# Making Q-hat and K-hat one turn earlier, with the gate row on GpSimd and value tiles that keep their zeros

## The chip, the cores and the metric

The kernel runs on one core of a Trainium2 chip. The metric is the device time of one execution in microseconds (us). The kernel before takes 488.94 us (median of 4 runs, 488.67 to 490.05).

Engine names: TensorE (PE, with its weight loads PEld), VectorE (DVE), ScalarE (ACT), GpSimd (POOL), SyncE (SP), which issues most transfers.

## The reference, cut to what matters

```python
# for each batch b, head h: a complex decay per position and feature
scale = np.minimum(mag, 0.999) / (mag + 1e-06)
a_re_n, a_im_n = a_re * scale, a_im * scale
for t in range(S):                                   # S = 768, D = 48, B = 4, H = 8
    new_re = ar * S_re - ai * S_im
    new_im = ar * S_im + ai * S_re
    S_re, S_im = new_re + k[t] (x) v[t], new_im
    y[t] = q[t] @ S_re
# then y, as 3072 rows of 384, goes through a mixture of 8 experts (one per row)
```

## The kernel before

The scan is done in chunks of 128 positions. A unit is one chunk of one batch (24 units); two units are a group. For each group the kernel makes logarithms and angles of the decays, sums them along the chunk with a triangular matmul (`ls` for the logarithms, `u` for the angles), and takes exponentials (`pm`, the moduli) and sines (`cs`). ScalarE needs one table of functions for exponentials and another for sines and arctangents (the traces show a table load of 1.28 us at each change), so these come in two blocks that alternate from turn to turn. VectorE multiplies them into q and k, which gives Q-hat and K-hat, the "hats". TensorE transposes the hats, forms their products `wp`, and multiplies these with V.

```python
    def hats(x, i):                    # group x, unit i of it
        P = un.tile([L, H, 2, D], F32, name="P")
        nc.vector.tensor_tensor(P[:], cs[:, i], both(pm[:, 0, i]), Alu.mult)
        kp = un.tile([L, H, D], F32, name="kp")
        nc.vector.tensor_tensor(kp[:], qk[:, 1, i], pm[:, 1, i], Alu.mult)
        for u in range(2):             # the last row of P is the gate of the whole chunk
            nc.sync.dma_start(out=c_scr[g * B + b, u][None], in_=P[L - 1:L]...)
        Qh = un.tile([L, H, 2, D], F32, name="Qh", bufs=3)
        nc.vector.tensor_tensor(Qh[:], P[:], both(qk[:, 0, i]), Alu.mult)
        KW = un.tile([L, H, C + L], F32, name="KW", bufs=5)
        nc.vector.tensor_tensor(KW[:, :, 0:C]..., cs[:, i], both(kp[:]), Alu.mult)
    # [cut]
    for w in range(NU + 1):            # one turn per unit
        unit(values, w + 1)            # loads of V and of the gate row, broadcast (cB)
        unit(turned, w + 2)            # transposes tKT, tQT on TensorE
        unit(inner, w + 1)             # wp, masked by VectorE into KW
        unit(outer, w)                 # py; U and the state update (GpSimd: t1, t2, state)
        unit(rows, w - 1)              # xw, xr
        if w % NG == 0:
            trigs(w // NG + 2)         # sines; arctangent; matmul sums u; squares
        else:
            exps(w // NG + 2)          # matmul sums ls; moduli pm; logarithms
        hat(w + 3)
```

The order in which the program names the operations is not quite the order on an engine. A scheduler puts each engine's operations in a fixed order before the run.

## Time and profile before

| | kernel before |
|---|---|
| time, 4 runs | 488.94 us (488.67 to 490.05) |
| span of the first profile | 467.5 us (this run itself: 469.34 us) |
| span of a second profile, other chip | 485.5 us |
| first product of the experts begins | 373.9 us, and 373.8 us |
| from there to the end | 93.6 us, and 111.7 us |
| TensorE waits at the transposes for K-hat | 46.9 us, and 47.4 us |

The prediction shows the views of the first profile that matter: busy shares, waits, the chain, and stretches of two turns each.

### The profile page before, as it was taken

The page shows a single profiled execution, that of the slowest core. Times are in us where ns is not written, and L with a number is a line of the kernel's source. Part 1 is how long each engine was busy: PE and PEld are TensorE (multiplying, and loading weights), DVE is VectorE, ACT ScalarE, POOL GpSimd, SP SyncE. Part 2 cuts the span into 40 slices and gives each one's busy share as a digit, 9 for nine tenths or more (in the row PEclk, how much of TensorE's full clock was granted, in tenths as well). Part 3 has the DMA queues.
Part 4 walks back from the last instruction along what each step waited for, and adds up shares of the span by engine and source line. Part 5 has one row for each costly group of instructions (what it writes and reads, how often), then busy time and mean ns, then how long its engine had stood idle before and what let it go on. Part 6 is the DMA issues. An engine that isn't in the chain of part 4 may idle for free.

```text
span 467.5 us, 8629 instructions
## 1 busy us (share of the span) xinstructions
PE 356.8 (76%) x3141; PEld 276.6 (59%) x3141; DVE 283.0 (61%) x563; ACT 263.7 (56%) x440; POOL 188.9 (40%) x218
## 2 busy tenths in 40 slices
PE   0356547386979879796969799796993199999994
PEld 0134415265767667674748577685882078777773
DVE  2586754657769687897766667946347034344441
ACT  3485956587869685866958675634521233333332
POOL 5521051634345445346332504133000647776542
PEclk9978777788898989797999979897997589999999
DMA  9949399289596969495919646517201999999991
GB/s 152 187 71 146 64 195 194 49 159 179 114 161 110 186 123 174 78 195 97 175 47 170 111 89 133 71 36 129 48 18 25 378 389 402 395 407 405 408 401 44
DMA packets 159500, 80.84 MB, mean 173 GB/s; under 512 B 135551, under 2 KB 149876, under 8 KB 159458
## 3 DMA queue, kind: packets, MB, share of 16 engines
q1 hardware_dynamic: 144466, 59.92, 52.1%
q0 software_dynamic: 14992, 20.37, 22.6%
q8 instruction: 25, 0.41, 0.4%
q14 instruction: 17, 0.14, 0.1%
HBM read 85.68 MB, written 21.12 MB: 228 GB/s over the span
## 4 chain that ended last, share of the span: by engine, by line
PE 58%; DVE 11%; issue 10%; ACT 8%; DMA 5%; POOL 4%; SPq 2%; POOLq 0%; DVEq 0%; ACTq 0%
PE wp L211 10%; PE py L235 8%; PE tKT L201 6%; PE h_ps L658 6%; PE tQT L201 5%; PE y_ps L669 5%; PE xw L263 5%; PE u L137 4%; PE py L238 4%; DVE KW L179 3%; PE tz L223 2%; POOL out_dram L677 2%; DMA ab<-in_a_im_dram 2%; DVE P L171 2%; DVE kp L173 2%
## 5 line engine op out<-in xcount | busy, mean ns | idle before, releaser
L201 PE MATMUL tKT<-ident,KW 128*96 128x128 f32 x192 | 35.9, 347 | 53.8 <-DVE KW L179 46.9
L201 PEld LDWEIGHTS tKT<-ident,KW 128*96 128x96 f32 x192 | 28.2, 161 | 63.6 <-issue 44.0
L235 PE MATMUL py<-KW,V 128*64 128x224 f32 x384 | 56.0, 358 | 0.0
L184 POOL MEMSET V<- 128x128 f32 x24 | 4.9, 207 | 121.2 <-PE py L235 121.2
L211 PE MATMUL wp<-QT,KT 96*64 96x128 f32 x768 | 53.2, 297 | 0.0
L211 PEld LDWEIGHTS wp<-QT,KT 96*64 96x64 f32 x768 | 47.4, 152 | 6.4 <-issue 2.9
L137 PE MATMUL u<-tan,turn 128*128 128x384 f32 x48 | 25.3, 615 | 34.0 <-ACT tan L82 34.0
L114 POOL TENSOR_SCALAR neg<-ab 128x768 bf16<-128x768 f32 x12 | 29.1, 2422 | 50.7 <-DMA ab<-in_a_re_dram 31.1
L635 POOL DMA_INDIRECT xg<-x_rows,idx x31 | 30.2, 974 | 42.2 <-ACT idx L619 33.0
L658 PE MATMUL h_ps<-xgT,w1t 128*128 128x256 bf16 (+1 forms) x456 | 45.5, 258 | 0.0
L212 DVE TENSOR_TENSOR KW<-wp,mask 128x512 f32<-128x512 f32 x48 | 32.6, 687 | 18.9 <-PE wp L211 18.7
L669 PE MATMUL y_ps<-w2t,hT 128*128 128x384 bf16 x248 | 43.5, 326 | 0.2 <-DVE hT L660 0.2
L662 ACT ACTIVATE hT<-h_ps 128x512 bf16<-128x512 f32 x31 | 18.5, 597 | 44.2 <-PE h_ps L658 44.2
L677 POOL DMA_INDIRECT out_dram<-y_sb,idx x31 | 31.2, 1007 | 29.6 <-ACT y_sb L673 24.4
L658 PEld LDWEIGHTS <-w1t 128*128 128x128 bf16 x456 | 38.9, 100 | 5.8
L202 ACT COPY KT<-tKT 96x512 f32<-96x512 f32 x48 | 27.0, 584 | 21.0 <-PE tKT L201 20.5
L238 PE MATMUL py<-QT,Zs 96*48 96x128 f32 x320 | 36.1, 275 | 0.0
L246 ACT COPY yT<-py 128x256 f32<-128x256 f32 x48 | 17.4, 372 | 32.3 <-DVE U L243 24.5
L79 ACT ACT_TABLE_LOAD x27 | 34.6, 1283 | 1.2 <-PEq L756 0.8
L201 PE MATMUL tQT<-ident,Qh 128*96 128x128 f32 x192 | 34.6, 341 | 0.1
L235 PEld LDWEIGHTS py<-KW,V 128*64 128x64 f32 x384 | 30.3, 136 | 6.7 <-issue 3.7
L171 DVE TENSOR_TENSOR P<-cs,pm 128x768 f32<-128x768 f32 x24 | 24.6, 1026 | 14.9 <-ACT pm L82 13.9
(135 smaller groups left out, 760.8 us busy)
## 6 DMA issues: line engine op xcount, KB each, us to landing
w1t<-w1b SPq DMA_DIRECT2D x19, 768.0 KB
w2t<-w2b SPq DMA_DIRECT2D x19, 768.0 KB
w1b<-in_moe_w_dram POOLq DMA_DIRECT2D x8, 768.0 KB, 7.7
w2b<-in_moe_w_dram POOLq DMA_DIRECT2D x8, 768.0 KB
ab<-in_a_re_dram SPq DMA_DIRECT2D x24, 192.0 KB
ab<-in_a_im_dram SPq DMA_DIRECT2D x24, 192.0 KB
qk<-in_q_dram SPq DMA_DIRECT2D x24, 192.0 KB
qk<-in_k_dram SPq DMA_DIRECT2D x24, 192.0 KB
```

The costliest lines, as they stand in the source:

```text
L79: then(nc.scalar.preload_act_table_set(name))
L137: nc.tensor.matmul(u, turn[:], tan[:, i], start=True, stop=False)
L171: nc.vector.tensor_tensor(P[:], cs[:, i], both(pm[:, 0, i]), Alu.mult)
L201: nc.tensor.transpose(tp[:, i, :], src[:, h4 + i], ident[:])
L211: nc.tensor.matmul(wp[u * 64:(u + 1) * 64, i, :], KT[:, h4 + i, u * 64:(u + 1) * 64], QT[:, h4 + i, :], start=True, stop=True)
L212: nc.vector.tensor_tensor(KW[:, h4:h4 + 4, C:], wp, mask[:, None, :].broadcast_to([L, 4, L]), Alu.mult)
L235: nc.tensor.matmul(py[u * 64:(u + 1) * 64, i, :], V[:, 2 * j + u, :], KW[:, 2 * j + u, :], start=True, stop=(g == 0))
L238: nc.tensor.matmul(py[u * 64:u * 64 + D, i, C:], Zs[:, j, u * 64:u * 64 + D], QT[:, 2 * j + u, :], start=False, stop=True)
L635: nc.gpsimd.indirect_dma_start(out=xg[:], out_offset=None, in_=x_rows, in_offset=bass.IndirectOffsetOnAxis(ap=idx[:, s, 0:1], axis=0))
L658: nc.tensor.matmul(h_ps[:, f, :], w1t[:, k, ff * 128:(ff + 1) * 128], xgT[:, k, :], start=(k == 0), stop=(k == KD - 1))
L669: nc.tensor.matmul(y_ps[:], hT[:, f, s * 128:(s + 1) * 128], w2t[:, f, :], start=(f == 0), stop=(f == NF - 1))
L677: sc = nc.gpsimd.indirect_dma_start(out=out, out_offset=bass.IndirectOffsetOnAxis(ap=idx[:, s, 1:2], axis=0), in_=y_sb[:], in_offset=None, ...
```

## The change

The intent was to take the chain moduli, hats, transposes off TensorE's path by making the hats a whole turn earlier, to pay for it with less work on VectorE (the narrow `qp` for the wide `P`), and to move the one thing that `P` was also good for, the gate row, to GpSimd, which was busy for 40% of the span. The value tiles keep their zero padding, so GpSimd need not clear it 24 times. Room comes from fewer buffers.

```diff
@@ -68,6 +68,11 @@
         return flat.rearrange(f"p ({names}) -> p {names}", **{f"x{i}": s for i, s in enumerate(shape[1:])})
 
 
+    Vs = [un.tile([L, H, 64], F32, name=f"V{i}", bufs=1) for i in range(3)]
+    for V in Vs:
+        nc.gpsimd.memset(V[:, :, D:64], 0.0)
+
+
     chain = []
 
     def then(ins):
@@ -167,21 +172,24 @@
         cs, pm = box["pm", x]
         qk = box["qk", x]
         g, b = groups[x][i]
-        P = un.tile([L, H, 2, D], F32, name="P")
-        nc.vector.tensor_tensor(P[:], cs[:, i], both(pm[:, 0, i]), Alu.mult)
+        qp = un.tile([L, H, D], F32, name="qp")
+        nc.vector.tensor_tensor(qp[:], qk[:, 0, i], pm[:, 0, i], Alu.mult)
         kp = un.tile([L, H, D], F32, name="kp")
         nc.vector.tensor_tensor(kp[:], qk[:, 1, i], pm[:, 1, i], Alu.mult)
-        for u in range(2):
-            nc.sync.dma_start(out=c_scr[g * B + b, u][None], in_=P[L - 1:L].rearrange("o (j u) c d -> o u j (c d)", u=2)[:, u])
-        Qh = un.tile([L, H, 2, D], F32, name="Qh", bufs=3)
-        nc.vector.tensor_tensor(Qh[:], P[:], both(qk[:, 0, i]), Alu.mult)
-        KW = un.tile([L, H, C + L], F32, name="KW", bufs=5)
+        Qh = un.tile([L, H, 2, D], F32, name="Qh", bufs=4)
+        nc.vector.tensor_tensor(Qh[:], cs[:, i], both(qp[:]), Alu.mult)
+        KW = un.tile([L, H, C + L], F32, name="KW", bufs=6)
         nc.vector.tensor_tensor(KW[:, :, 0:C].rearrange("t h (c d) -> t h c d", c=2), cs[:, i], both(kp[:]), Alu.mult)
+        if g < G - 1:
+            c = un.tile([L, H, 2, D], F32, name="c", bufs=1)
+            end = slice(L - 32, L)
+            nc.gpsimd.tensor_tensor(c[end], cs[end, i], pm[end, 0, i][:, :, None, :].broadcast_to([32, H, 2, D]), Alu.mult)
+            for u in range(2):
+                nc.sync.dma_start(out=c_scr[g * B + b, u][None], in_=c[L - 1:L].rearrange("o (j u) c d -> o u j (c d)", u=2)[:, u])
         box["hats", g, b] = Qh, KW
 
     def values(g, b):
-        V = un.tile([L, H, 64], F32, name="V", bufs=3)
-        nc.gpsimd.memset(V[:, :, D:64], 0.0)
+        V = Vs[(g * B + b) % 3]
         nc.sync.dma_start(out=V[:, :, 0:D], in_=at(v, g, b))
         cB = None
         if g < G - 1:
@@ -353,10 +363,10 @@
         unit(outer, w)
         unit(rows, w - 1)
         if w % NG == 0:
-            trigs(w // NG + 2)
+            exps(w // NG + 2)
         else:
-            exps(w // NG + 2)
-        hat(w + 3)
+            trigs(w // NG + 3)
+        hat(w + 4)
         marks.append(chain[-1])
         if casts and w % 3 != 2:
             cast = casts.pop(0)()
# [cut: tan, neg and lm from three buffers to two; the prologue; the iota tile]
```

The prologue gets `hat(3)` and `trigs(2)` before the first turn. Cut from the diff: the iota tile of the router, shortened to 32 numbers.

More of the change, by code (lines that the diff above doesn't have):

```diff
@@ L110, in squares @@
         act(sq[:], ab[:], Act.Square)
-        tan = el.tile([L, NG, H, D], F32, name="tan", bufs=3)
+        tan = el.tile([L, NG, H, D], F32, name="tan", bufs=2)
         nc.vector.tensor_tensor(tan[:], ab[:, 0], ab[:, 1], Alu.mult)
-        neg = el.tile([L, NG, H, D], BF16, name="neg", bufs=3)
+        neg = el.tile([L, NG, H, D], BF16, name="neg", bufs=2)
         nc.gpsimd.tensor_scalar(neg[:], ab[:, 0], 0.0, None, Alu.is_lt)
@@ L120, in logs @@
         sq, tan, neg = box.pop(("squares", x))
-        lm = el.tile([L, NG, H, D], F32, name="lm", bufs=3)
+        lm = el.tile([L, NG, H, D], F32, name="lm", bufs=2)
         act(lm[:], sq[:, 1], Act.Ln)
@@ L346, in gate_loop @@
     load_qk(2)
+    hat(3)
+    trigs(2)
     marks = [chain[-1]]
@@ L423, in __init__ @@
         W = max(self.NC, 128)
-        self.io = rc.tile([TP, W], F32, name="io")
-        nc.gpsimd.iota(self.io[:], pattern=[[1, W]], base=0, channel_multiplier=0, allow_small_or_imprecise_dtypes=True)
+        self.io = rc.tile([TP, 32], F32, name="io")
+        nc.gpsimd.iota(self.io[:], pattern=[[1, 32]], base=0, channel_multiplier=0, allow_small_or_imprecise_dtypes=True)
         self.iob = rc.tile([TP, W], BF16, name="iob")
-        nc.gpsimd.tensor_copy(self.iob[:], self.io[:])
+        nc.gpsimd.iota(self.iob[:], pattern=[[1, W]], base=0, channel_multiplier=0, allow_small_or_imprecise_dtypes=True)
         self.p1 = rc.tile([TP, 1], F32, name="p1")
```

## The prediction

> **What bounds the kernel now.** I read the page first for the busy shares:
>
> ```profile
> PE 356.8 (76%) x3141; PEld 276.6 (59%) x3141; DVE 283.0 (61%) x563; ACT 263.7 (56%) x440; POOL 188.9 (40%) x218
> ```
>
> No engine is full, so waits decide. The last 93 us (374 to 467) are the expert layers, which the diff leaves alone. The change lies in the gate loop before them, so next I asked for the longest waits:
>
> ```profile
> POOL V L184 <- PE py L235: 121.2, 19, 13.4
> PE tKT L201 <- DVE KW L179: 46.9, 10, 7.8
> ```
>
> Columns: total us, number of waits, longest. The first is GpSimd standing at the clearing of a value tile until the products three units back have let go of it; in the chain it does not appear, and a load of V only once after 100 us (2.90 us at 262.90). The second is TensorE standing still, about once in two turns (a turn is one unit of 128 positions of one batch; the kernel has 24). Two more of these waits, 6.9 us, carry the name of a router operation on VectorE. The chain shows how one comes about:
>
> ```profile
> 213.69 0.46 ACT pm L82
> ...
> 214.18 1.00 DVE P L171
> 215.18 0.86 DVE kp L173
> ...
> 216.14 1.09 issue
> 217.23 1.58 DVE KW L179
> ...
> 218.86 1.94 PE tKT L201 x8
> 220.80 1.71 PE tQT L201 x8
> ...
> 231.08 0.87 PE tKT L201 x8
> 231.95 0.87 PE tQT L201 x8
> ```
>
> Columns: start, length, what. ScalarE makes the moduli, VectorE the products P, kp, Qh (hidden in "issue") and KW, and only then may TensorE transpose K-hat. TensorE is idle for 4.59 us here. In the next turn, 12 us later, K-hat is long there and the same transposes start with no wait. They also run at 0.87 us for eight instead of 1.94 and 1.71: after the gap TensorE runs at half speed. Then I cut the loop at the start of each waited-for transpose, so a stretch is two turns:
>
> ```profile
> 166.06:190.39 24.33, 21.22 (x210) 17.01 (x210) 20.62 (x45) 18.25 (x32) 8.54 (x12) 0.92 0.91 157
> 190.39:218.86 28.47, 23.81 (x211) 18.92 (x211) 24.49 (x58) 19.63 (x32) 15.71 (x15) 0.86 0.71 131
> 218.86:244.64 25.78, 21.72 (x195) 17.18 (x195) 18.30 (x28) 18.75 (x30) 9.52 (x12) 0.90 0.57 102
> 244.64:269.53 24.89, 20.83 (x194) 16.46 (x195) 17.04 (x27) 18.70 (x31) 9.62 (x12) 0.91 0.81 136
> ```
>
> Columns: stretch, us, then busy us of PE, PEld, DVE, ACT and POOL, granted clock, DMA share, GB/s. From 91.81 to 320.48 there are nine such pairs, 228.7 us, so 25.4 us each. PE is busy 192.2 us of them by the same view: 36.4 us idle, 4.0 per pair.
>
> **What the Trainium skill says.**
> "TensorE: Matmul & The Clock Gate", section "What's actually happening", says that the array clock halves after about an idle window of 3.4 us and comes back after about as long of work. The trace agrees: a gap of 4.59 us, then transposes at 0.24 us each against 0.11 when warm.
> "SBUF — State Buffer", section "Who interferes with whom", says that a VectorE instruction with two SBUF inputs contends with a GpSimd instruction that reads SBUF, while one from PSUM does not. The trace agrees: P, kp, Qh and KW take 0.95, 0.55, 0.95 and 0.95 us at 28 to 31 us with GpSimd idle, and 1.38, 1.35, 1.34 and 1.34 us at 86 to 91 us beside GpSimd's state products.
> "GPSIMD Engine Reference", section "Extended-addressing connectivity", says that for tensor_tensor each core works on its own 16 partitions. So 32 partitions instead of 128 should save no time; the trace has no such product on few partitions to test this.
>
> **The change part by part.**
> *Hats one turn ahead.* Before, the moduli of a group of two units came in an odd turn, the hats of its first unit after them, and the next turn began with the transposes of those hats. Now the moduli come in the even turn, the hats of unit w+4 after them, and their transposes are still two turns later: a whole turn, about 10 us, lies between, against a chain of about 5 us. The bound on what this can give: the idle 4.0 us per pair, plus the slow clock after it: (1.91 - 0.87) + (1.71 - 0.87) for the transposes and some 0.8 on the wp products (2.4 to 3.0 us after gaps, 1.9 else), so 2.7. A pair would be 25.4 - 4.0 - 2.7 = 18.7 us if TensorE alone counted.
> *Two products instead of the wide ones.* P (128x768) becomes qp (128x384). On an undisturbed VectorE these are 0.95 and 0.55 us (kp has the shape of qp), so 0.4 us a unit, 0.8 a pair, off VectorE.
> *Gate row on GpSimd.* Twenty products of 768 elements a partition. GpSimd's state products of 384 take 1.00 and 1.15 us (rows L251, L252), so about 2.0 us each: 40 us in all, 4 us a pair. GpSimd goes from 10.6 us a pair (mean of the first eight) to about 14.5 of 22: it fits. But it reads SBUF, so VectorE pays: in the stretch of 86 to 91.7 us the four products took 5.1 us instead of 3.1 while GpSimd worked 4.8 us, about 0.4 us for each us of overlap. Half overlapped, c costs VectorE 4 x 0.5 x 0.4 = 0.8 us a pair. It eats what qp saves.
> *Value tiles with their zeros.* Removes 24 clearings of 0.2 us, 4.9 us of GpSimd off the path, and the stand of 121 us with it, so the state products and casts behind start when their own inputs are there. The loads of V still wait for the old readers. By itself I give this about 0.
> *Buffers, rows of numbers.* tan, neg and lm go to two buffers; by program order only two are alive. One good side effect: at 84.39 us VectorE stood 3.5 us for the load of a tile whose product had been put early into its queue; fewer buffers let fewer such products run ahead. The iota of 32 numbers: below 1 us.
> *Prologue.* Trigonometry of group 2 and hats 3 move ahead of turn 0. The trace shows that the hats of unit 3 already run at 53 to 57 us, before turn 0's products: little really moves there. I count 0 to 4 us of loss, since loads and casts already crowd that time (DMA share 1.08 from 60 to 79 us).
>
> What remains per pair after the gap: PE 18.7; DVE 19.0 (mean of eight pairs) - 0.8 + 0.8 = 19.0; ACT 18.6. Three engines at about 19 us, each in order and waiting for the others, do not reach 19. The turns without a gap give a measure: 218.86 to 231.08 less its 2.7 of slow clock is 9.5, 231.08 to the end of its moduli sums at about 241.0 is 9.9 us, so 19.4 a pair, but there VectorE and ScalarE had the gap to catch up in. I choose 22.2 us: PE at 84%, DVE and ACT at 85%. That is the chosen number in this sum. Saving: 9 x (25.4 - 22.2) = 29 us; less 3 us for the prologue: 26. Span 467.5 - 26 = 441.5; with the 21.5 us by which the timed median lies above the profiled span, 463 us.
>
> **The rivals.**
> *VectorE or ScalarE becomes the bound.* For it: in the two pairs with much router work VectorE is already at 20.6 and 24.5 us busy, and GpSimd's reads are going to lengthen it. Against: in the others it is 17 to 19. If the pairs came out at 24, the saving is 9 x 1.4 = 13 us: 476.
> *A longer queue on SyncE and GpSimd.* The write of the gate row now waits for GpSimd's c, which stands behind the state update and, every other turn, behind neg (2.4 us), which waits for a load (31.1 us in eight waits). SyncE issues in order, so V, cB and the a loads stand behind it; and the single pm buffer can't be refilled until c has read it. For it: SyncE already waits 44.2 us for xr and 41 us for py. Against: the loads are issued about two turns ahead. If half the gap came back as load waits: 478; all of it and the contention: 490.
> *The full prize.* TensorE back to back, warm: pairs of 20 us, 9 x 5.4 = 49 us: 440.
> *DMA bound.* Shares of 0.8 to 0.94 per pair at 25 us become 0.92 to 1.08 at 22, which has been seen at 60 to 79 us. It could hold early pairs at 24, while casts run: about 5 us lost. That is within the range.
>
> **Range and chances.** The prize needs only that a static lead of one turn holds, and a spare of 10 against 5 us is ample; its size is the doubt. From 20.3 to 24.2 us a pair gives 446 to 479. Faster by 2% means below 479.2, a pair under 24.0 with the prologue's loss: 0.83. Within 2%: 0.14. Slower: 0.03, only for the SyncE queue.
>
> **What would show it.** Right: the wait of tKT for KW falls from 46.9 to under 10 us; no pair of transpose groups near 1.9 and 1.7 us in the loop after 100 us; pairs at 21 to 23 us with PE clock above 0.95; c at about 2.0 us; qp at 0.6 to 0.7 us; no wait at V on GpSimd; kp, Qh and KW means up by up to 0.1 us. Wrong: the transposes still wait, now for Qh or KW behind router work or contention; ScalarE's pm waiting for GpSimd's c; SyncE's c_scr issue waiting for c with V late at py; or the gap simply standing elsewhere, at ScalarE's copies or U.

## More of the kernel before

Two chips turned up, and on one of them the last part of a kernel, the expert layers, is about 18 us shorter.

## The result, and the profile after

The changed kernel takes 509.96 us (median of 4 runs, 506.76 to 513.06) against 488.94 us. The ratio is 1.0425, with a 95% interval of 1.0353 to 1.0497. Here and below, ratios are the mean time of one kernel's runs over that of the other's of the same rounds, so not quite the ratio of the medians. The change made the kernel 4% slower; 5% faster had been predicted.

The busy shares of the changed kernel, which answer to the first fence of the prediction:

```profile
PE 361.7 (72%) x3141; PEld 268.9 (53%) x3141; DVE 296.7 (59%) x563; ACT 258.1 (51%) x440; POOL 224.7 (45%) x217
```

VectorE should have got less work, and its busy time went up from 282.6 us (second profile of before) to 296.7. GpSimd got 35.7 us more. The waits of the changed kernel, longest first, as far as they matter (total us, times, longest):

```profile
PE u L142 <- ACT tan L87: 82.9, 12, 19.7
...
POOL c L186 <- DMA c_scr<-c: 19.0, 7, 4.1
...
PE tKT L209 <- DVE KW L182: 7.9, 1, 7.9
```

The wait that the change was made for is gone. The 46.9 us at the transposes became one wait of 7.9 us, in the prologue. In its place TensorE stands before the angle sums `u` and waits for ScalarE's arctangent: 82.9 us in 12 waits, of which one of 19.7 is the start of the kernel. In the kernel before (second profile) the same two waits were:

```profile
PE tKT L201 <- DVE KW L179: 47.4, 10, 8.1
PE u L137 <- ACT tan L82: 34.1, 5, 19.8
```

Four of the five waits at `u`, 32.6 us, lay in the first 80 us. The two kinds of stand together are 81.5 us before and 90.8 after.

Where the loss lies shows at `xw`, a product that comes once a turn. The first one starts at 94.6 us against 81.5, so 13.1 us are lost before the loop is under way. From the first to the last one it takes 273.6 us against 270.5, so only 3.1 are lost in the loop.

The chain of the changed kernel shows where the arctangent is stuck (start, length, what):

```profile
148.07 2.12 DVE Qh L180
150.19 0.28 DVE U L251
150.46 0.02 issue
150.49 0.37 ACT yT L254
150.86 0.81 ACT cs L87 x2
...
152.69 0.75 ACT tan L87
...
153.48 1.65 PE u L142 x2
```

It reads as follows. VectorE makes a hat, late. Behind it in VectorE's order stands `U`, which ScalarE's copy `yT` waits for. Behind the copy in ScalarE's order stand the sines and the arctangent. TensorE has finished its own work of the turn at 148.75, the end of its last product before `u`, and stands for 4.73 us. (The chain gives a piece only the time that it adds; `Qh` itself lasts from 148.07 to 150.19.) The next transposes, whose hats have long been ready, stand behind `u` in its order.

Two turns of the changed kernel, cut at the start of `u` (stretch, us, busy us of PE, PEld, DVE, ACT, POOL, granted clock, DMA share, GB/s):

```profile
126.23:153.48 27.25, 20.98 (x194) 15.81 (x194) 19.37 (x27) 18.24 (x31) 16.30 (x13) 0.94 0.70 131
153.48:181.20 27.72, 22.61 (x195) 17.13 (x195) 19.38 (x27) 18.25 (x31) 14.50 (x13) 0.87 0.73 133
```

The six pairs from 126.23 to 296.44 us take 28.4 us each on average ((296.44 - 126.23) / 6), against 25.4 before. This is the slow middle of the loop: over the whole loop the two kernels differ by only the 3.1 us given above, since the changed kernel's first and last turns are shorter.

Why is VectorE late? In part because of GpSimd. While the `Qh` of the chain above takes 2.12 us (0.94 where nothing disturbs it), GpSimd makes the gate row:

```profile
147.57 1.80 POOL L186 TENSOR_TENSOR c<-cs,pm 32x768 f32<-32x768 f32 x1 [2.94 <-DVE lm L132]
```

The clearest case is in the prologue, with VectorE and GpSimd side by side (start, length, engine, line, operation, tiles):

```profile
27.54 0.56 DVE L176 TENSOR_TENSOR qp<-qk,pm 128x384 f32<-128x384 f32 x1 [2.94 <-ACT pm L87]
27.65 2.11 POOL L186 TENSOR_TENSOR c<-cs,pm 32x768 f32<-32x768 f32 x1 [2.38 <-ACT pm L87]
28.02 2.17 DVE L178 TENSOR_TENSOR kp<-qk,pm 128x384 f32<-128x384 f32 x1
```

`kp` has the same shape as `qp` and takes about 0.55 us alone. It starts while GpSimd makes `c`, which ends at 27.65 + 2.11 = 29.76, and it ends itself at 28.02 + 2.17 = 30.19, which is 0.43 us later. So nearly all of its work came after `c` was through. In the groups this shows as a longer mean (busy us, mean ns); first the kernel before (second profile), then the changed kernel:

```profile
L179 DVE TENSOR_TENSOR KW<-cs,kp 128x768 f32<-128x768 f32 x24 | 23.7, 986 | 0.0
L182 DVE TENSOR_TENSOR KW<-cs,kp 128x768 f32<-128x768 f32 x24 | 35.2, 1468 | 0.0
```

### The profile page after: what moved, and what is told of

Read it like the earlier page. It is cut to its first block, busy times and chain, and to the rows that moved or that the text cites. A ratio compares the mean times of both kernels' runs of the same rounds, so it can differ in the third digit from the quotient of the medians.

```text
span 504.8 us, 8653 instructions
## 1 busy us (share of the span) xinstructions
PE 361.7 (72%) x3141; PEld 268.9 (53%) x3141; DVE 296.7 (59%) x563; ACT 258.1 (51%) x440; POOL 224.7 (45%) x217
## 4 chain that ended last, share of the span: by engine, by line
PE 42%; DVE 19%; ACT 16%; issue 9%; DMA 5%; POOL 3%; SPq 3%; DVEq 1%; another core or an unknown queue 1%; POOLq 0%; ACTq 0%
PE u L142 6%; PE h_ps L668 6%; PE y_ps L679 6%; PE py L243 5%; PE wp L219 5%; PE xw L271 3%; ACT sq L87 3%; DVE kp L178 3%; ACT pm L87 3%; DVE lm L132 2%; PE tKT L209 2%; PE py L246 2%; ACT cs L87 2%; DVE Qh L180 2%; ACT L84 2%
## 5 line engine op out<-in xcount | busy, mean ns | idle before, releaser
L142 PE MATMUL u<-tan,turn 128*128 128x384 f32 x48 | 37.2, 879 | 82.9 <-ACT tan L87 82.9
L243 PE MATMUL py<-KW,V 128*64 128x224 f32 x384 | 59.8, 373 | 10.0 <-DVE KW L220 9.9
L142 PEld LDWEIGHTS u<-tan,turn 128*128 128x128 f32 x48 | 13.9, 324 | 92.9 <-ACT tan L87 68.4
L186 POOL TENSOR_TENSOR c<-cs,pm 32x768 f32<-32x768 f32 x20 | 43.4, 2170 | 40.3 <-DMA c_scr<-c 19.0
L259 POOL TENSOR_TENSOR t<-U,cB 128x384 f32<-128x384 f32 x20 | 22.6, 1130 | 83.5 <-issue 49.4
L679 PE MATMUL y_ps<-w2t,hT 128*128 128x384 bf16 x248 | 47.2, 335 | 7.5 <-ACT hT L672 4.3
L668 PE MATMUL h_ps<-xgT,w1t 128*128 128x256 bf16 (+1 forms) x456 | 46.9, 260 | 7.3 <-DVE hT L670 3.8
L645 POOL DMA_INDIRECT xg<-x_rows,idx x31 | 30.1, 972 | 46.9 <-ACT idx L629 37.8
L219 PE MATMUL wp<-QT,KT 96*64 96x128 f32 x768 | 47.2, 276 | 0.0
L219 PEld LDWEIGHTS wp<-QT,KT 96*64 96x64 f32 x768 | 41.4, 137 | 4.7 <-issue 3.6
L220 DVE TENSOR_TENSOR KW<-wp,mask 128x512 f32<-128x512 f32 x48 | 32.6, 683 | 10.6 <-PE wp L219 10.6
L670 DVE TENSOR_SCALAR hT<-h_ps 128x512 bf16<-128x512 f32 x31 | 21.4, 692 | 27.9 <-PE h_ps L668 13.8
L679 PEld LDWEIGHTS <-hT 128*128 128x128 bf16 x248 | 22.8, 100 | 25.9 <-ACT hT L672 8.0
```

The costliest lines, as they stand in the source:

```text
L142: nc.tensor.matmul(u, turn[:], tan[:, i], start=True, stop=False)
L186: nc.gpsimd.tensor_tensor(c[end], cs[end, i], pm[end, 0, i][:, :, None, :].broadcast_to([32, H, 2, D]), Alu.mult)
L219: nc.tensor.matmul(wp[u * 64:(u + 1) * 64, i, :], KT[:, h4 + i, u * 64:(u + 1) * 64], QT[:, h4 + i, :], start=True, stop=True)
L220: nc.vector.tensor_tensor(KW[:, h4:h4 + 4, C:], wp, mask[:, None, :].broadcast_to([L, 4, L]), Alu.mult)
L243: nc.tensor.matmul(py[u * 64:(u + 1) * 64, i, :], V[:, 2 * j + u, :], KW[:, 2 * j + u, :], start=True, stop=(g == 0))
L668: nc.tensor.matmul(h_ps[:, f, :], w1t[:, k, ff * 128:(ff + 1) * 128], xgT[:, k, :], start=(k == 0), stop=(k == KD - 1))
```

## The experiments

Twelve kernels were run, each with three rounds against the kernel before. All gave correct results. The landmark is the start of the first product of the experts in the profile; it does not contain the part that differs between chips. It is read from one execution each, and the timed runs of one kernel spread by 0.5 to 6.3 us (the changed kernel most, and its profile is of its fastest run), so a difference of landmarks of a few us is rough.

| kernel | time, us | before in the same call | ratio (95% interval) | first expert product |
|---|---|---|---|---|
| kernel before (second profile) | 487.13 | 489.14 | 0.996 (0.991 to 1.001) | 373.8 |
| changed kernel | 509.96 | 488.94 | 1.0425 (1.035 to 1.050) | 390.2 |
| lead_no_gate | 480.66 | 489.14 | 0.9805 (0.976 to 0.985) | 362.5 |
| gate_only | 514.84 | 489.14 | 1.0525 (1.048 to 1.057) | 400.5 |
| rest_only | 488.29 | 489.14 | 0.9977 (0.994 to 1.002) | 374.5 |
| idle_read | 485.37 | 469.86 | 1.033 (1.029 to 1.037) | 388.1 |
| idle_write | 469.60 | 469.86 | 0.9975 (0.995 to 1.000) | 376.1 |
| gate_on_vector | 475.96 | 469.86 | 1.0126 (1.010 to 1.016) | 380.0 |
| lead_late_u | 426.36 | 469.86 | 0.9052 (0.902 to 0.909) | 330.0 |
| before_late_u | 485.13 | 488.94 | 0.9923 (0.987 to 0.998) | 369.1 |
| after_late_u | 469.66 | 488.94 | 0.9581 (0.952 to 0.964) | 355.1 |
| gate_three_tiles | 509.74 | 488.94 | 1.0414 (1.036 to 1.047) | 394.0 |
| lead_late_u_small_gate | 445.43 | 488.94 | 0.9103 (0.906 to 0.915) | 331.9 |

Two theories stood at the start. Theory 1: the gate product on GpSimd holds VectorE, and everything behind VectorE comes late. Theory 2: the gate is harmless, and the lead itself only moved TensorE's stand from the transposes to `u`.

### The kernel before again

No edit.

> The kernel before, unchanged, for a second profile. Its timed runs were 489 us, its first profiled run only 469, and in the changed kernel the part from the first up-product of the experts to the end took 114 us against 93 in that first profile. Theory A (the first profile of before caught a quick execution): this profile has a span near 487, the gate loop again ends near 352, and the expert part takes about 113. Theory B (the change slows the expert part): the expert part takes about 93 whenever it is looked at and the 20 us lie elsewhere.

Measured: a span of 485.5 us, and 111.7 us from the first product of the experts at 373.8 to the end. That is theory A: the first profile of before was a quick one. The granted clock in the expert part is 0.98 in both, so the clock is not what differs. In the changed kernel the part takes 114.6 us on a slow chip, 2.9 us more than before. So most of the change's loss lies before it: 390.2 against 373.8, 16.4 us.

### The lead without the gate on GpSimd

```diff
 # against the changed kernel
-        qp = ...; nc.vector.tensor_tensor(qp[:], qk[:, 0, i], pm[:, 0, i], Alu.mult)
+        P = ...;  nc.vector.tensor_tensor(P[:], cs[:, i], both(pm[:, 0, i]), Alu.mult)
-        nc.gpsimd.tensor_tensor(c[end], cs[end, i], ..., Alu.mult)   # and its write
+        # the gate row is the last row of P again
```

> The changed kernel with the wide product P back on VectorE and no gate product on GpSimd: lead, kept zeros and buffers stay. Theory 1 (GpSimd's gate product holds VectorE, so U, yT and the arctangent come late): below 487 us, ratio to before under 0.995, KW<-cs,kp back at about 0.98 us. Theory 2 (the lead itself only moved TensorE's stand from the transposes to the angle sums u): 500 to 512 us, TensorE still waits about 80 us for the arctangent.

Measured: 480.66 us, ratio 0.9805 (clear of 1, but at the 2% line the record calls it unclear), and KW<-cs,kp at a mean of 1057 ns against 1468. By the time theory 1 is right: the gate costs 27.7 us at the landmark (390.2 - 362.5). But half of theory 2 holds too:

```profile
PE u L142 <- ACT tan L87: 72.9, 12, 18.5
```

This wait hardly fell, from 82.9 to 72.9 us. So the lead does move the stand. It still gains a little: the two kinds of stand come to 79.4 us (72.9 and 6.5) against 81.5, and 6.8 us at the transposes for a router operation (`own`) are gone too.

### Only the gate on GpSimd

```diff
 # against the kernel before: hats() as in the change, Qh and KW with their old buffers
+        qp = ...; nc.vector.tensor_tensor(qp[:], qk[:, 0, i], pm[:, 0, i], Alu.mult)
+        nc.gpsimd.tensor_tensor(c[end], cs[end, i], pm[end, 0, i]..., Alu.mult)
```

> The kernel before with only qp and the gate product on GpSimd. Theory 1: 498 to 512 us, KW<-cs,kp at 1.3 to 1.5 us, and the stand at the transposes longer than 47 us. Theory 2: 485 to 492 us, since without the lead nothing moves on TensorE.

Measured: 514.84 us, 26.7 us later at the landmark than the kernel before, and the wait of the transposes for KW went from 47.4 to 63.2 us. KW<-cs,kp has a mean of 1216 ns, a little below the range expected. The gate alone (with what `qp` saves set against it) costs as much here as it does under the lead, so the two parts of the change add up: -11.3 us for the lead and +26.7 for the gate make +15.4, and the whole change has +16.4.

### Only the rest

```diff
 # against the kernel before
+    Vs = [un.tile([L, H, 64], F32, name=f"V{i}", bufs=1) for i in range(3)]   # cleared once
-    tan, neg, lm with bufs=3
+    tan, neg, lm with bufs=2         # and the short iota
```

> The kernel before with only the kept zeros, two buffers for tan, neg and lm, and the short iota. Both theories: 486 to 492 us. A third theory (fewer buffers keep products of the next group from running early): 495 us or more.

Measured: 488.29 us, ratio 0.9977. Kept zeros and fewer buffers are free and worth nothing, as predicted.

### What of the gate costs: its reads, its time or its chain

idle_read adds the same product to the full kernel before (with `lm` on two buffers to make room, as in rest_only), into a tile that nobody reads, so nothing waits for it to be written or loaded. idle_write puts clearings of about the same length in its place, which read nothing.

```diff
 # idle_read, against the kernel before
+            nc.gpsimd.tensor_tensor(idle[end], cs[end, i], pm[end, 0, i]..., Alu.mult)
 # idle_write, against the kernel before: three of these, the first tied to the end of P
+            nc.gpsimd.memset(idle[L - 32:L], 0.0)
```

> The kernel before, all of it, plus the same GpSimd product cs times pm on 32 partitions into a tile that nobody reads (lm on two buffers for room). gate_only was 25.7 us slower than before. Theory 1a (GpSimd's reads hold VectorE): most of it is here too, 500 to 515 us, KW<-cs,kp above 1.2 us. Theory 1b (what hurts is the chain product to write to load on SyncE and the single tile of c): 487 to 494 us.

> The kernel before plus three GpSimd clearings of 768 numbers on 32 partitions per unit, started after P, into a tile that nobody reads: about as long as the gate product, but without reads. Theory 1a: 487 to 493 us, P, Qh and KW as in before, since only reads hold VectorE. A theory 1c (GpSimd's time itself delays the state and neg behind it): as slow as idle_read.

(The numbers expected for these and the next two were written for the slower chip, where before takes 489 us; on this one it takes 470. The differences from before are what counts.) Measured: idle_read is 15.5 us slower than before, ratio 1.033. idle_write is equal to it, ratio 0.9975, though GpSimd is as busy: 233.0 us in idle_read and 233.4 in idle_write, against 189.0 in before. The same group of VectorE's products, first in idle_read, then in idle_write:

```profile
L179 DVE TENSOR_TENSOR KW<-cs,kp 128x768 f32<-128x768 f32 x24 | 30.3, 1264 | 0.0
```

```profile
L179 DVE TENSOR_TENSOR KW<-cs,kp 128x768 f32<-128x768 f32 x24 | 23.7, 987 | 0.0
```

VectorE is busy 310.1 us with the reading products beside it, 283.2 us with the writing ones and 282.6 us without either. So the twenty products hold it for 27.5 us, 1.4 us each. Theory 1a is shown for these 15.5 us of the 25.7 that gate_only lost, and theory 1c (GpSimd's time itself) falls.

### The gate product on VectorE

```diff
 # against gate_only
-            nc.gpsimd.tensor_tensor(c[end], ...)
+            nc.vector.tensor_tensor(c[end], ...)
```

> gate_only with the gate product of 32 partitions on VectorE instead of GpSimd; qp, the single tile of c and its write stay. It costs VectorE about 0.9 us a unit and saves 0.4, so 0.5 more than before. Theory 1a: 486 to 496 us. Theory 1b: above 500 us, since the chain over the single tile stays.

Measured: 6.1 us slower than before, ratio 1.0126, at the upper side of what theory 1a allowed (3 us less to 7 more than before). The product takes 0.97 us on VectorE and 2.17 on GpSimd, and even so VectorE is the better place for it: at the landmark gate_only is 20.5 us later than this kernel.

### Three tiles for the gate

```diff
 # against gate_only; to make room also tan, neg, lm with bufs=2 and the short iota, as in rest_only
-            c = un.tile([L, H, 2, D], F32, name="c", bufs=1)
+            c = un.tile([L, H, 2, D], F32, name="c", bufs=3)
```

> gate_only with three tiles for c instead of one (tan, neg, lm and the iota made smaller for room, which rest_only showed to be free). gate_only was at a ratio of 1.0525, idle_read at 1.033. If GpSimd's standing for the write of the single tile (39.5 us in gate_only) makes that difference: 1.03 to 1.04, and no wait of c for c_scr. If not: 1.045 to 1.06.

Measured: ratio 1.0414, landmark 394.0, 6.5 us earlier than gate_only; the wait of `c` for its own write, 39.5 us in gate_only, is gone. It fell just outside the range that was to decide for the single tile, and outside the other one too. At the landmark the hold on VectorE alone costs 14.3 us (idle_read: 388.1 - 373.8) of the gate's 26.7. The rest is not cleanly divided. Without the stand for its write `c` runs earlier and holds VectorE more (busy 299.6 us, against 290.8 in gate_only), so the 6.5 us are the single tile less this. And SyncE's queue, which stands 65.8 us for `c` in gate_only with loads behind it, is seen on gate_only's chain once: VectorE stands 8.94 us, until 234.19, for a load of `a` (3.9 us at the most in the kernel before, after 80 us). With three tiles no such wait is left, so part of what the single tile cost may have gone through that queue. In the changed kernel VectorE waits for no load longer than 1.1 us from 80 us to the experts. VectorE's own work also differs between these kernels by the narrow `qp`.

### The angle sums one turn later

If TensorE stands at `u` only because `u` comes before the next transposes in its order, it helps to let it do them first. The arctangent stays where it is. Its matmul and the rounding after it go one turn later in program order, behind `turned` and `inner`.

```diff
 # against lead_no_gate
-        if x + 1 < NX:
-            angles(x + 1)            # arctangent, matmul u, rounding
+        if x + 1 < NX:
+            arcs(x + 1)              # arctangent only
 ...
         unit(turned, w + 2)
         unit(inner, w + 1)
+        if w % NG == 0:
+            sums(w // NG + 3)        # matmul u, rounding
         unit(outer, w)
```

> lead_no_gate with the angle sums u put one turn later in program order, behind the transposes and the products wp, so that TensorE need not stand for the arctangent. lead_no_gate was 480.7 us with TensorE waiting 72.9 us for the arctangent, 18.5 of it at the very start. If that wait is what is left of the gap: 462 to 474 us, the wait under 45 us. If ScalarE's order sets the pace anyway, the stand moves on to another instruction and the time stays at 477 to 483 us.

Measured: 426.36 us against 469.86 in the same call, ratio 0.9052. That is 43.5 us faster than before, more than either branch had expected. Its busy shares, its wait at `u`, and a stretch of its loop:

```profile
PE 339.3 (80%) x3141; PEld 256.8 (60%) x3141; DVE 288.1 (68%) x563; ACT 256.0 (60%) x440; POOL 193.4 (46%) x197
```

```profile
PE u L149 <- ACT tan L87: 42.5, 5, 18.7
```

```profile
110.00:280.00 170.00, 159.68 (x1573) 121.06 (x1574) 155.38 (x298) 134.40 (x231) 86.22 (x79) 0.98 0.83 152
```

From 110 to 280 us TensorE is busy 159.7 of 170 us (94%), at a granted clock of 0.98; before it was 192.2 of 228.7 us (84%) at 0.90, from 91.81 to 320.48. VectorE is at 155.4 of 170 (91%). A pair of turns, taken between the starts of the moduli at 139.78 and 268.73 us with six pairs between, takes 21.5 us. The gaps are nearly gone, and so is most of the slow clock that followed them. (The edit moves VectorE's rounding along with the matmul; the two were not tried apart.) From the first to the last product `xw` the loop takes 221.7 us (86.1 to 307.8) against 270.5 before (81.5 to 352.0).

### The later sums without the lead

The same move in the kernel before.

```diff
 # against the kernel before; arcs in place of angles, as above
+        if w % NG == 1:
+            sums(w // NG + 3)
```

> The kernel before with only the angle sums u moved one turn later, behind the transposes and wp; no lead. If the lead and the later sums work only together: within 1.5% of before, since TensorE still stands at the transposes for KW, about 45 us. If the place of the sums alone is the whole gain of lead_late_u (a ratio of 0.905): below 0.95.

Measured: ratio 0.9923, 4.7 us at the landmark. TensorE still stands at the transposes for KW, 54.1 us. Each move alone gives little: 11.3 us for the lead, 4.7 for the later sums. Together they give 43.8 (373.8 - 330.0). With only one of them TensorE stands once in two turns all the same, at one place or the other.

### The whole change with the later sums

```diff
 # against the changed kernel: the edit of lead_late_u
```

> The changed kernel with its gate product on GpSimd kept, and the angle sums moved as in lead_late_u. With VectorE now the chain of lead_late_u, its being held by GpSimd's reads should cost at least as much as in the kernel before (25.7 us): ratio to before 0.95 to 0.98. If the cost came only through the arctangent that was late for TensorE: ratio under 0.93.

Measured: ratio 0.9581, inside the range expected. It is 25.1 us later at the landmark than lead_late_u (355.1 - 330.0), so the gate product on GpSimd (with its write and the narrow `qp`) costs 25 to 28 us in all three settings in which it was tried: 26.7 alone, 27.7 under the lead, 25.1 here.

### A small gate product

lead_late_u with the narrow `qp`, as the change wanted it. The gate row is made of two rows that transfers bring onto 8 partitions; the product is of 96 numbers on each.

```diff
 # against lead_late_u
-        P = ...                                       # wide product
+        qp = ...                                      # narrow product
+            nc.sync.dma_start(out=rows2[:, 0:2], in_=cs[L - 1:L, i]...)
+            nc.sync.dma_start(out=rows2[:, 2], in_=pm[L - 1:L, 0, i])
 # one turn later:
+        nc.vector.tensor_tensor(c[:], rows2[:, 0:2], rows2[:, 2:3]..., Alu.mult)
```

> lead_late_u with the narrow qp, and the gate row made of two rows brought by DMA onto 8 partitions, a product of 96 numbers each on VectorE (about 0.15 us) one turn later, nothing on GpSimd. VectorE is saved about 0.4 - 0.15 us a unit and is the chain now: 24 units, 4 to 8 us faster than lead_late_u, ratio to before 0.885 to 0.90. If the extra small transfers hold up SyncE's queue: 0.905 to 0.93.

Measured: 445.43 us against 488.94, a gain of 43.5 us, the same as that of lead_late_u on the other chip; the landmark is 1.9 us later. The gain expected from the narrow product was not there. VectorE's busy time fell by only 4.3 us (288.1 to 283.8), less than the 6 us that 24 times 0.25 would be; the small product took 0.35 us (mean of 20), where 0.15 had been expected. The ratio of 0.9103 lies in the range of the second branch (transfers holding up SyncE's queue), but this doesn't show that cause: a gain of 43.5 us is a ratio of about 0.91 on the slower chip anyway. The two kernels never ran on the same chip, so nothing finer can be said. lead_late_u, the simpler of the two, stays the best version found.

## Why the prediction was wrong

It foresaw 463 us (446 to 479) and gave "slower" a chance of 0.03. The time was 509.96. Its steps in turn:

**What bounds the kernel.** Right as far as it went. The wait for K-hat was real, and the lead removed it, as the prediction said it would. Two small slips in its sums: over the first seven gaps of its chain the transposes and `wp` are 2.3 us slower a pair, not 2.7; and with its 3 us for the prologue the upper end of its range, 24.2 us a pair, gives 481 and not 479.

**Hats one turn ahead.** This step failed in part. The prediction asked whether the hats would be there in time; it did not ask what TensorE would wait for next. Its order puts `u` before the next transposes, and the arctangent stands behind copies and sines in ScalarE's order. In the kernel before, TensorE waited only 1.5 us at `u` after the first 80 us; that ScalarE got ahead while TensorE stood at the transposes is the likely reason, and was not tested apart. The prediction listed it only as the last of the things that would make it wrong ("the gap simply standing elsewhere"). Instead of 29 us the loop gained 18.9 by the lead alone (first to last `xw`: 251.6 us in lead_no_gate against 270.5), and the prologue lost 7.5 us (first `xw` at 89.0 against 81.5) where 0 to 4 had been allowed. With the order mended, in lead_late_u, a pair takes 21.5 us, near the prediction's 22.2 (and 28.4 in the middle of the changed kernel). So a prize of that size was there; but 22.2 was a chosen number, and that it came so near is partly luck.

**Gate row on GpSimd.** This is the step that turned a small gain into a loss. The durations were right: 2.17 us for about 2.0, and 32 partitions saved no time. The sum failed at "about 0.4 us for each us of overlap. Half overlapped, c costs VectorE 4 x 0.5 x 0.4 = 0.8 us a pair". Twenty such products held VectorE for 27.5 us in idle_read, which is 1.4 us each and 2.7 us a pair, more than three times the term. Both factors were too small. Not half but about nine tenths of `c` lies beside VectorE's products of two SBUF tiles: 40 of its 44.7 us in idle_read and 40 of 43.4 in the changed kernel (summed here over the rows of the timelines). And 27.5 us for 40 us of overlap is about 0.7, not 0.4. The slope came from one stretch with GpSimd's four shorter operations on the state; that VectorE finds room between those is the likely reason, not shown. Beside one product of 2.1 us `kp` came out 1.6 us late.

The overlap is not only a common start: in 4 of 20 cases `c` starts within 0.35 us of the moduli that the hats also wait for, in the others 0.8 to 8.3 us later, and mostly it still meets a product. About half of the hold (14.3 of 27.5 us) came out at the landmark. The prediction's own sign failed too: it allowed kp, Qh and KW 0.1 us more, and their means went from 0.73, 1.06 and 0.99 us to 0.90, 1.23 and 1.47. What `qp` saves (0.4 us a unit, and at 0.56 against 0.96 us undisturbed it does) is small beside that.

In the loop the gate took back the 18.9 us of the lead and 3.1 more, and before it added 5.6 us to the lead's 7.5. So between the 26 us that were to be saved and the 16.4 that were lost at the landmark lie 14.7 us of the lead (11.3 for 26) and 27.7 of the gate.

**Value tiles and buffers.** Right: rest_only is at 0.9977.

**The rival of SyncE's queue.** The prediction reckoned 478 to 490 us for it. The queue is there: SyncE stood 47.2 us for `c` in the changed kernel. But the hold on VectorE alone is 14.3 of the gate's 26.7 us, with no queue in it, and in the changed kernel VectorE waits for no load longer than 1.1 us in the loop. How much of the other 12 us goes through the queue stays open; gate_only shows one such stand, of 8.94 us.

**The 21.5 us between profile and time.** The prediction took them for a constant. The profiled run itself took 469.34 us, 1.8 us over its span; nearly all of the rest was the expert part on another chip. It shifted the centre of the prediction by nothing that mattered, since both kernels were timed on the slow chip.

## What to carry to other kernels

When a wait is taken away from an engine that works in a fixed order, read what stands next in that order and what it waits for. A lead pays in full only when the next stand is moved too; here two moves of 11.3 and 4.7 us were worth 43.8 together. Work for an "idle" GpSimd is not free when it reads SBUF at the moment at which VectorE multiplies two SBUF tiles: here each such product of about 2.2 us held VectorE for 1.4 us on average and for 1.6 at the clearest, and nine tenths of their time fell beside VectorE's products. Look in the timeline for what would stand beside the new instruction before calling the overlap a half.

## What the Trainium skill lacked or had wrong

- "SBUF — State Buffer", section "Who interferes with whom", has it right, and the prediction used too little of it. It says that the shared port pair is an exclusive lock, and that a GpSimd instruction that only writes does not disturb a VectorE instruction with two SBUF inputs; that page's section "Summary: rules for kernel authors" adds that of such a pair the second one to issue blocks until the first is through. This agrees on all three: VectorE was busy 27.5 us longer for twenty reading products; with clearings instead it was busy 283.2 us against 282.6; and `kp` took 2.17 us instead of 0.55 beside a product of 2.11 us. What the page lacks is a measured share for a stream of mixed work: here 1.4 us of hold for each product of 2.2 us, about half of which reached the end of the loop.
- "GPSIMD Engine Reference", section "Engine selection", puts GpSimd at about twice VectorE's time for two inputs. This agrees: 2.17 us on average against 0.97 for the same product, and 1.80 in gate_only at 125.94 us, where no VectorE product of two SBUF tiles ran beside it. Fewer partitions did not shorten it, as the prediction had taken from the same page: 32x768 took 2.17 us and 128x384, half the numbers per partition, 1.05 to 1.13.
- No page that was read mentions that one kernel's expert layers can take 93.6 us on one chip and 111.7 on another, at one granted clock of 0.98 and with the same bytes moved. The cause was not looked for.
